# Attention with an exact-Gelu MLP on one core: four raw weight pieces in flight instead of two, half of them staged in the turning buffers, and other portions of the MLP in the second batch

## Chip, cores, metric

One Trainium2 chip, one core. The metric is the device time of one execution in microseconds. A single execution's trace can differ from the next in its first 40 us by some microseconds (first loads), so totals are compared by medians over several runs, and traces by what happens inside them.

## The reference, cut to what matters

```python
# q, k, v: (8 batches, 8 heads, 576, 64) float32; tau = 0.02
scores = scale * np.matmul(q, k.transpose(0, 1, 3, 2))
thresh = np.max(scores, axis=-1, keepdims=True) - tau
scores = np.where(scores >= thresh, scores, -1000000000.0)
attn = exp(scores - max); attn = attn / (sum + 1e-09)
x = (attn @ v) as (4608 tokens, 512)
h = x @ w_in                       # w_in (512, 2048), handed in as float64
g = 0.5 * h * (1.0 + erf(h * inv_sqrt2))
return g @ w_out                   # w_out (2048, 512), handed in as float64
```

The weights come as 64-bit words; the kernel takes the words apart with integer steps and puts float32 together. That is done in 32 pieces of 128 x 512 values.

## The kernel before

The work is a row of *slots*. A pair of heads has five (four of 128 query rows for both heads, one for the tails), a batch has 20: slots 0 to 19 are batch 0, 20 to 39 batch 1. Each slot emits scores on TensorE, the softmax on VectorE and ScalarE, then some steps of the weights' conversion, then a portion of the MLP on TensorE. The order in the program is the order on each engine.

```python
    xg = ctx.enter_context(tc.tile_pool(name="xg", bufs=7))       # raw pieces AND blocks of x
    pd = [const.tile([P, 4 * KR, P], FP32, name=f"pd{e}") for e in range(2)]   # turning buffers
    # ...
    def load_piece():
        # ...
        raw, shifted = (xg.tile([P, 2 * PIECE], U32, tag="x", name=s) for s in ("raw", "shifted"))
        nc.gpsimd.dma_start(raw, src.bitcast(U32))
        n = 8 * PIECE - 4
        nc.gpsimd.dma_start(shifted.bitcast(U8)[:, 0:n], src.bitcast(U8)[:, 3:3 + n])
        raws.append((dst, raw, shifted))

    def conversions():
        ahead = None
        while raws or ahead:
            piece = None
            if raws:
                # ... expo of piece k+1 (VectorE), power of piece k+1 (ScalarE)
                vec.tensor_scalar(expo, hi, 0x7FF00000, None, op0=ALU.bitwise_and)
                nc.scalar.activation(power, expo, AF.Relu, bias=rebias, scale=8.0)
                piece = dst, hi, top, power
                yield 450
            if ahead:
                # ... mant, power, product of piece k (VectorE); then the next load is emitted
                vec.tensor_scalar(mant, top, 0x0FFFFFFF, 0x10000000, op0=ALU.bitwise_and, op1=ALU.bitwise_or)
                yield 450
                vec.scalar_tensor_tensor(power, hi, 0x80000000, power, op0=ALU.bitwise_and, op1=ALU.bitwise_or)
                yield 720
                vec.scalar_tensor_tensor(dst, mant, 2.0 ** -28, power.bitcast(FP32), op0=ALU.mult, op1=ALU.mult)
                load_piece()
                converted[0] += 1
                yield 720
            ahead = piece

    # turn_p, late batches: the weights p of a slot are turned into pd; after the fourth slot
    # pd is stored to DRAM, from where it comes back in another order
        to = pd_tail[p % 2] if i == NC else pd[e][:, :, i * Q:(i + 1) * Q]
        nc.vector.transpose(to[:, 0:NB, :], w[:, e * S:(e + 1) * S].rearrange("p (b i) -> p b i", i=Q))
    # ...
    goal = [0.0] + [1.5 + 2.08 * i for i in range(B - 1)]     # blocks of the MLP done by the end of a batch
    for n in range(len(slots) + WEIGH + 1):
        # ... scores, softmax_head, turn_p of the slot before, softmax_tail, loads
        if n < BATCH:
            convert(2300)
        elif batch < 2:
            convert(9000)
        if n >= BATCH:
            done = min(batch, B - 1)
            fill((goal[done] - goal[done - 1]) * BLK_NS / (BATCH if done > 1 else BATCH), weighed // HP)
```

`convert(ns)` runs conversion steps until their estimated times (the yields) sum to ns; `fill(ns)` does the same with the matmuls of the MLP. A block of the MLP is 256 tokens: 64 hT matmuls, eight Gelus, 32 o_ps matmuls (the trace has two instructions for each float32 matmul).

Names in the profile: sc are scores, p the weights that softmax makes of them, hT and o_ps the first and the second product of the MLP, g its Gelu; raw and shifted are the two copies of a piece's words that are loaded, expo, mant and power the steps of its conversion (exponent bits, mantissa bits, signed power of two).

## Time and profile before

| | before |
|---|---|
| median of 4 runs beside the changed kernel | 1530.50 us (1530.03 to 1532.71) |
| span of the profiled run | 1528.7 us |
| TensorE busy | 94% |
| TensorE idle up to slot 19 / slots 19 to 24 / slots 24 to 39 | 36.1 / 41.6 / 8.2 us |

The last row is the sum of the gaps that TensorE's timeline shows ahead of its lines, split at the scores of the tail slots. After slot 39 there are none, so idle time before it (and slow-clock time that follows idle time) is what this change can win. The prediction shows the lines themselves.

### The profile page before, as it was taken

What the parts mean: (1) busy time and instruction counts of PE and PEld (TensorE: products, weight loads), DVE (VectorE), ACT (ScalarE), POOL (GpSimd) and SP (SyncE); (2) the same over time, 40 slices, a digit from 0 to 9 for tenths busy, and PEclk for the clock granted to TensorE, in tenths of its full rate; (3) what the DMA queues carried; (4) which work ended last, traced back from release to release, by engine and by line L of the source; (5) the groups of instructions that cost most, each with busy time, mean ns of one, the idle gap of its engine ahead of it and who ended that gap; (6) DMA issues with size and microseconds to landing.
All of it is one profiled execution on the core that took longest, in us unless ns stands there. A gap on an engine that the chain in (4) does not pass through costs nothing.

```text
span 1528.7 us, 17454 instructions
## 1 busy us (share of the span) xinstructions
PE 1438.7 (94%) x6092; PEld 897.3 (59%) x6092; DVE 899.7 (59%) x2089; ACT 643.3 (42%) x934; POOL 40.9 (3%) x84
## 2 busy tenths in 40 slices
PE   6875558999999999999999999999999999999999
PEld 4443444665656565757565757575747474765764
DVE  6997566667676667676776666667666666000000
ACT  5775364563535252625362635262626252100110
POOL 3112100000000000000000000000000000000000
PEclk9888679999999999999999999999999999999999
DMA  9665457777666667676776767666666655500000
GB/s 257 177 201 183 146 157 180 186 179 187 175 170 177 179 162 185 174 198 172 182 185 180 183 173 181 152 167 169 178 179 174 172 150 147 144 14 7 7 14 14
DMA packets 398887, 237.61 MB, mean 155 GB/s; under 512 B 230352, under 2 KB 380880, under 8 KB 391632
## 3 DMA queue, kind: packets, MB, share of 16 engines
q1 hardware_dynamic: 391632, 202.96, 51.5%
q0 software_dynamic: 7168, 33.54, 6.5%
q8 instruction: 49, 0.80, 0.2%
q14 instruction: 38, 0.31, 0.1%
HBM read 144.43 MB, written 92.01 MB: 155 GB/s over the span
## 4 chain that ended last, share of the span: by engine, by line
PE 82%; issue 9%; DMA 3%; POOL 2%; ACT 1%; DVE 1%; SPq 0%; POOLq 0%; DVEq 0%; ACTq 0%
PE o_ps L430 32%; PE hT L419 31%; PE sc L313 10%; PE xT L391 9%; DMA shifted<-in_moe_w_in_dram 1%; POOL raw L136 1%; DMA turned<-pd 1%; POOL shifted L138 1%; DVE p L338 1%; SPq L366 0%; DMA shifted<-in_moe_w_out_dram 0%; ACT L325 0%; ACT L423 0%; ACT p L347 0%; DVE nmx L324 0%
## 5 line engine op out<-in xcount | busy, mean ns | idle before, releaser
L419 PE MATMUL hT<-x,w_in 128*128 128x256 f32 x2304 | 525.1, 385 | 11.8 <-ACT x L400 11.8
L430 PE MATMUL o_ps<-w_out,g 128*128 128x512 f32 x1152 | 515.3, 599 | 0.0
L419 PEld LDWEIGHTS hT<-x,w_in 128*128 128x128 f32 x2304 | 438.2, 192 | 100.5 <-issue 27.9
L324 DVE TENSOR_REDUCE nmx<-sc 128x1 f32<-128x576 f32 x288 | 206.2, 752 | 298.7 <-PE sc L313 297.6
L430 PEld LDWEIGHTS o_ps<-w_out,g 128*128 128x128 f32 x1152 | 215.1, 190 | 259.7 <-issue 256.9
L325 ACT ACTIVATE p<-sc,nmx 128x576 f32<-128x576 f32 x288 | 202.6, 741 | 335.8 <-DVE nmx L324 335.4
L338 DVE SCALAR_TENSOR_TENSOR p<-sc,thr,p 128x576 f32<-128x576 f32 x288 | 220.2, 796 | 19.4 <-ACT p L325 18.0
L313 PE MATMUL sc<-kT,qT 64*128 64x288 f32 x1024 | 183.3, 448 | 33.0 <-DVE p L338 32.8
L313 PEld LDWEIGHTS sc<-kT,qT 64*128 64x128 f32 x1024 | 102.0, 194 | 117.5 <-issue 100.2
L361 DVE STREAM_TRANSPOSE pd<-p 128x576 f32<-128x576 f32 x224 | 161.8, 757 | 10.7 <-DMA turned<-pd 10.7
L391 PE MATMUL xT<-pT,v 128*64 128x288 f32 x1280 | 165.9, 413 | 0.0
L423 ACT ACTIVATE g<-hT 128x512 f32<-128x512 f32 x144 | 85.0, 597 | 125.7 <-PE hT L419 124.8
L391 PEld LDWEIGHTS xT<-pT,v 128*64 128x64 f32 x1280 | 89.9, 139 | 76.5 <-issue 18.3
L349 DVE TENSOR_SCALAR p<-p,rden 128x576 f32<-128x576 f32 x216 | 103.6, 518 | 4.2
L423 ACT ACT_TABLE_LOAD x75 | 96.2, 1283 | 12.7 <-PE hT L419 11.6
L325 ACT ACT_TABLE_LOAD x74 | 94.9, 1283 | 1.6 <-DVE nmx L324 0.2
L400 ACT COPY x<-xT 128x256 f32<-128x256 f32 (+7 forms) x128 | 29.2, 282 | 152.3 <-PE xT L391 152.2
L433 ACT COPY o_sb<-o_ps 128x512 f32<-128x512 f32 x36 | 21.0, 584 | 147.7 <-PE o_ps L430 147.7
L347 ACT ACTIVATE p<-p,rden 128x576 f32<-128x576 f32 x72 | 52.4, 770 | 54.9 <-DVE rden L343 54.2
L313 PE MATMUL sc<-kT,q_tail 128*128 128x288 f32 x128 | 43.7, 468 | 30.2 <-DVE p L338 30.2
L313 PEld LDWEIGHTS sc<-kT,q_tail 128*128 128x128 f32 x128 | 23.7, 206 | 47.4 <-issue 43.3
L159 ACT ACTIVATE power<-expo,rebias 128x512 uint32<-128x512 uint32 x32 | 22.9, 717 | 46.2 <-DVE expo L158 46.2
(58 smaller groups left out, 431.1 us busy)
## 6 DMA issues: line engine op xcount, KB each, us to landing
pT<-turned SPq DMA_DIRECT2D x56, 1440.0 KB, 7.8
turned<-pd SPq DMA_DIRECT2D x224, 320.0 KB, 5.2
out_dram<-o_sb SPq DMA_DIRECT2D x36, 256.0 KB, 2.2
turned<-pd_tail SPq DMA_DIRECT2D x112, 80.0 KB, 2.9
raw<-in_moe_w_in_dram POOLq DMA_DIRECT2D x16, 512.0 KB, 5.1
raw<-in_moe_w_out_dram POOLq DMA_DIRECT2D x16, 512.0 KB, 3.9
shifted<-in_moe_w_in_dram POOLq DMA_DIRECT2D x16, 511.5 KB, 5.3
shifted<-in_moe_w_out_dram POOLq DMA_DIRECT2D x16, 511.5 KB, 4.5
```

Of the source, the lines that this page charges most:

```text
L313: nc.tensor.matmul(sc[e][:, h, 0:HALF], lhsT=lhsT, rhs=s["kT"][rows, at:at + HALF], start=True, stop=True)
L324: nc.vector.tensor_reduce(nmx[:, e:e + 1], sc, axis=AXIS.XY, op=ALU.max, negate=True)
L325: nc.scalar.activation(w[:, e * S:(e + 1) * S].rearrange("p (h s) -> p h s", h=2), sc, AF.Exp, bias=nmx[:, e:e + 1], scale=1.0)
L338: nc.vector.scalar_tensor_tensor(row, sc[e][:, :, 0:HALF], thr[:, e:e + 1], row, op0=ALU.is_ge, op1=ALU.mult, accum_out=den[:, e:e + 1])
L347: nc.scalar.activation(row, row, AF.Copy, bias=0.0, scale=rden[:, e:e + 1])
L349: nc.vector.tensor_scalar(row, row, rden[:, e:e + 1], None, op0=ALU.mult)
L361: nc.vector.transpose(to[:, 0:NB, :], w[:, e * S:(e + 1) * S].rearrange("p (b i) -> p b i", i=Q))
L391: nc.tensor.matmul(xT[f, 0:HALF], lhsT=s["v"][:, e, c, :], rhs=pT[:, c, cols], start=(c == 0), stop=(c == KR - 1))
L400: nc.scalar.copy(x_blk[n][:, hp, o:o + size], xT[:, at - lo:at - lo + size])
L419: nc.tensor.matmul(hT[:, j % 2, :], lhsT=w_in_sb[c][:, j * P:(j + 1) * P], rhs=x_blk[n][:, c, :], start=(c == 0), stop=(c == N_DM - 1))
L423: nc.scalar.activation(t, hT, AF.Gelu)
L430: nc.tensor.matmul(o[:, 0:d_model], lhsT=g[j][:, m * P:(m + 1) * P], rhs=w_out_sb[j], start=(j == 0), stop=(j == N_DF - 1))
```

## The change

Its intent: keep VectorE supplied with raw weights, so that 24 of 32 pieces are converted in batch 0, and give TensorE its first half block of the MLP early. The pool of seven tiles cannot hold four raw pieces (eight tiles) beside three blocks of x. The turning buffers are not needed before slot 21, so every second of the first 24 pieces is staged there.

```diff
+    EARLY_PIECES = 24
@@ load_piece
-        raw, shifted = (xg.tile([P, 2 * PIECE], U32, tag="x", name=s) for s in ("raw", "shifted"))
+        k = loaded[0] - 1
+        if k % 2 and k < EARLY_PIECES:
+            room = pd[k // 2 % 2][:, 0:NB - 2, :].bitcast(U32).rearrange("p b i -> p (b i)")
+            raw, shifted = room[:, 0:2 * PIECE], room[:, 2 * PIECE:4 * PIECE]
+        else:
+            raw, shifted = (xg.tile([P, 2 * PIECE], U32, tag="x", name=s) for s in ("raw", "shifted"))
@@ conversions: estimates of the steps 450, 450, 720, 720 -> 340, 340, 720, 700
@@ before the slots
-    for _ in range(2):
+    for _ in range(4):
         load_piece()
@@ in the slots
-        if n < BATCH:
-            convert(2300)
-        elif batch < 2:
-            convert(9000)
-        if n >= BATCH:
+        if batch == 0:
+            convert(EARLY_PIECES * 2100 / BATCH)
+        elif n < BATCH + 2:
+            convert(1e12 if n > BATCH else 9000)
+        if batch:
             done = min(batch, B - 1)
-            fill((goal[done] - goal[done - 1]) * BLK_NS / (BATCH if done > 1 else BATCH), weighed // HP)
+            share = (goal[done] - goal[done - 1]) * BLK_NS / BATCH
+            if batch == 1:
+                share = BLK_NS / 8 if n < BATCH + 4 else (share * BATCH - BLK_NS / 2) / (BATCH - 4)
+            fill(share, weighed // HP)
```

More of the change, by code (lines that the diff above doesn't have):

```diff
@@ L160, in conversions @@
                 piece = dst, hi, top, power
-                yield 450
+                yield 340
             if ahead:
@@ L165, in conversions @@
                 vec.tensor_scalar(mant, top, 0x0FFFFFFF, 0x10000000, op0=ALU.bitwise_and, op1=ALU.bitwise_or)
-                yield 450
+                yield 340
                 vec.scalar_tensor_tensor(power, hi, 0x80000000, power, op0=ALU.bitwise_and, op1=ALU.bitwise_or)
@@ L171, in conversions @@
                 converted[0] += 1
-                yield 720
+                yield 700
             ahead = piece
```

## The prediction

> **What bounds the kernel now.** I read the page's 40 slices first, then busy time in stretches of 20 us, then the waits of the first 320 us, then the timelines of VectorE and TensorE where the stretches show trouble. The slices come first because the averages of the span hide two regimes:
>
> ```profile
> PE   6875558999999999999999999999999999999999
> DVE  6997566667676667676776666667666666000000
> PEclk9888679999999999999999999999999999999999
> ```
>
> One digit is 38 us. From the ninth slice on TensorE is full; only before it, in some 310 us, can time be had. The change touches only this part: attention of batch 0, conversion of the 32 weight pieces (their float64 words are turned into float32 on VectorE, with one step on ScalarE), and the slots of batch 1. Stretches:
>
> ```profile
> 120.00:140.00 20.00, 12.44 (x63) 8.03 (x63) 17.24 (x44) 11.76 (x20) 3.22 (x6) 0.83 0.66 188
> 140.00:160.00 20.00, 8.21 (x39) 5.38 (x37) 11.35 (x25) 5.79 (x12) 4.40 (x8) 0.72 0.59 198
> 160.00:180.00 20.00, 12.18 (x53) 9.59 (x51) 10.36 (x22) 5.78 (x8) 3.75 (x7) 0.84 0.52 184
> 180.00:200.00 20.00, 8.87 (x28) 6.50 (x28) 10.22 (x22) 7.13 (x10) 3.31 (x7) 0.67 0.30 105
> 240.00:260.00 20.00, 20.00 (x86) 9.54 (x86) 13.30 (x32) 8.62 (x17) 0.00 (x0) 1.00 0.48 101
> ```
>
> Columns after the length: busy us of PE, PEld, DVE, ACT, POOL, then granted clock, DMA share, GB/s. Up to 140 VectorE is the bound (17 to 19 of 20 us from 40 on). Between 140 and 205 nothing is: VectorE half idle, TensorE half idle and slow, DMA far from full. That is a chain of latencies, and the waits name it:
>
> ```profile
> POOL raw L136 <- DVE mant L165: 123.6, 24, 14.4
> DVE expo L158 <- DMA raw<-in_moe_w_out_dram: 26.7, 10, 3.9
> ```
>
> One turn of the chain in VectorE's timeline:
>
> ```profile
> 145.03 0.43 DVE L158 TENSOR_SCALAR expo<-raw 128x512 uint32<-128x512 uint32 x1 [2.87 <-DMA raw<-in_moe_w_out_dram]
> 145.37 0.42 DVE L165 TENSOR_SCALAR mant<-shifted 128x512 uint32<-128x512 uint32 x1
> 145.70 0.69 DVE L167 SCALAR_TENSOR_TENSOR power<-raw,power 128x512 uint32<-128x512 uint32 x1
> 146.42 0.69 DVE L169 SCALAR_TENSOR_TENSOR w_out<-mant,power 128x512 f32<-128x512 uint32 x1
> 149.90 0.43 DVE L158 TENSOR_SCALAR expo<-raw 128x512 uint32<-128x512 uint32 x1 [2.78 <-DMA raw<-in_moe_w_out_dram]
> ```
>
> Two pieces are in flight, but the order on VectorE is expo of piece k+1 before mant of piece k. Only mant frees the buffer for load k+2, and expo of k+2 is the very next thing after piece k. So each load is waited for in full: 4.87 us a piece, of which 2.8 is waiting. TensorE hangs on this, in order:
>
> ```profile
> 156.36 10.56 PE L419 MATMUL hT<-x,w_in 128*128 128x256 f32 x34 [11.79 <-ACT x L400]
> 183.98 2.99 PE L313 MATMUL sc<-kT,qT 64*128 64x288 f32 x8 [11.81 <-DVE p L338]
> 208.93 2.26 PE L313 MATMUL sc<-kT,q_tail 128*128 128x288 f32 x4 [16.08 <-DVE p L338]
> ```
>
> These three gaps are 39.7 us. After 216 idle time on TensorE comes to only some 8 us more (0.78, 0.99, 1.01, 3.68, 0.19, 1.51).
>
> **What the Trainium skill says.** (1) "DMA: Bandwidth & Descriptors", Anatomy of one DMA (SWDGE path): some 2.0 us fixed plus bytes over 436e3 per us, so 3.2 us for a raw half of 512 KB. The trace has 3.8 us as its least and 4.1 as its median from issue to landing of raw: a little slower, same order, and mostly latency, so depth is the right cure. (2) Same page, Queues, rings and completion order: each engine takes turns between queue rows, packet by packet. So a deeper weight queue takes turns from the q, k, v loads; the trace agrees in that the k load of pair 1 is waited for until 28.8 us while DMA share is 0.9 to 1.1. (3) "TensorE: Matmul & The Clock Gate", What's actually happening: after an idle window the array runs at half clock until it has been busy. The trace agrees: the same eight sc matmuls take 2.99 us at 184 and 1.24 us at 253.7. Gaps cost more than their length. (4) "Perfetto Trace Analysis", Optimization Strategy: a bubble that recurs unchanged can mean too few buffers; the 2.8 us bubble is that.
>
> **The change, part by part.** Slots are numbered 0 to 19 for batch 0, 20 to 39 for batch 1.
>
> *More conversion in batch 0.* From the order of instructions: when slot 20's softmax ends, 24.2 pieces are through VectorE instead of 19.7. A piece takes 1.94 us start to start (expo 0.34, mant 0.34, power 0.6 to 0.7, product 0.6). 4.5 x 1.94 = +8.7 us on the engine that bounds this part. Small waits for raw disappear there (0.40, 0.59, 0.20, 0.51, 0.28: -2.0). The first loads now are 4 MB rather than 2 MB beside q, k, v on a saturated DMA: I allow +2 us. Slot 20's softmax ends at 139.5 + 8.7 = 148 instead of 139.5.
>
> *Fewer pieces afterwards, but not deeper.* From piece 24 on everything is in the pool of 7 again, of which 3 hold x; four pieces in flight would need 8. The order of GpSimd's DMA issues with their waits shows it: load 25 waits for the buffers of piece 22, 26 for 24's, 27 for 25's, up to 31 for 29's. So 24 and 25 are there in time, and 26 to 31 run at the old cadence, 4.87 us each. Waits of 2.8 us: 6 instead of 9. Laid out: expo 26 at 152.9, 27 at 157.8, 28 at 162.6, 29 at 167.5; slot 21's softmax (4.8 us as before) to 172.7; expo 30 at 177.2, expo 31 at 182.1, the last two products to 185.7. Before, the last product ended at 211.2, after slot 23's softmax. Four conversions now stand between slots 20 and 21 as before did three, and ScalarE's copy of x is behind five power steps in order: the first hT starts at about 169 (before 156.4).
>
> *Larger portions.* An eighth of a block per slot for slots 20 to 23 rather than 0.075: 16 matmuls (32 instructions; the trace has two per matmul) instead of some 10. At slot 21 two portions are due: 64 instructions from 169, at 0.31 us cold for the first 34 as at 156.4 and 0.23 after, to 187. Then slots 22 and 23: 1.24 for sc and 7.3 us for 32 hT each, longer than VectorE's 5 to 7 us, so TensorE has no gap. sc of slot 24 starts at 203.7 with 128 hT done (before 208.9 with 78), sc of slot 25 at about 208.7 with the work of 144 (before 216.25 with 96). Lead: 7.5 us + 48 x 0.23 = 18.5 us.
>
> *Smaller portions in slots 24 to 39.* 0.0625 block instead of 0.075: 3.6 us instead of 4.6 a slot. Now the serial chain of a slot bounds more of them. Where a Gelu stands in it the trace's period is 7.44 us:
>
> ```profile
> 222.88 1.94 PE L313 MATMUL sc<-kT,qT 64*128 64x288 f32 x8 [0.78 <-DVE p L338]
> ...
> 230.31 1.94 PE L313 MATMUL sc<-kT,qT 64*128 64x288 f32 x8 [0.99 <-DVE p L338]
> ```
>
> Eight of the 16 slots hold a Gelu (hT of block 1), eight hold o_ps. TensorE's work in slots 25 to 39: sc 18.6, xT 15.2, MLP 15 x 3.6 = 54, sum 88 us; before 103 less the MLP difference of 15, that is 98 warm, and it took 114 (216.25 to 330). The chain makes it some 99 to 106 now. So idle plus cold time there is 11 to 18 against 16 before: between +5 and -2 of the lead is kept or lost.
>
> *Sum.* Lead 18.5 us, less 4 us for slots 25 to 39 and for what I may have put too early in the first 40 us. Gain about 14 us. From slot 40 on TensorE is full in both kernels and emits the same work, so the lead goes through to the end: 1530 - 14 = 1516 us.
>
> **The rivals.** *The whole serial stretch goes*: if four pieces really were in flight up to the last, the six waits (17 us) would go too, and time would be near 1499. The intent speaks for it; the buffers' waits in the instruction order speak against it. *The bound moves and nothing is won*: VectorE pays 8.7 us more up front and DMA contention delays pair 1's k more than I allow; slots 25 to 39 turn chain-bound at 7.4 us each (16 x 7.4 + 3 x 3 = 127 us would be worse than before). VectorE's 95% busy share in 40 to 60 us speaks for the first; that the slots with o_ps ran at 5.7 us speaks against the second. It would give 1524 to 1530. *The portions alone do it*: the new loads bring nothing net, since 8.7 us up front eats the saved waits (3 x 2.8 = 8.4), and the gain is only the hT done early in slots 20 to 23, which would otherwise stand still. By my own sum this is nearly so; it gives the same 1512 to 1520, but says where the gain is from.
>
> **Range and chances.** Batch 0's end is uncertain by 4 us, slots 25 to 39 by 6, slot 20 to 24 by 4; as independent errors about 8 us. That gives 1506 to 1526. Over 2% faster means below 1499.4, which needs the first rival: 0.06. Over 2% slower would need a new stall of 45 us: 0.01. Within 2%: 0.93.
>
> **What would show it right or wrong.** Right: six waits of expo for raw of 2.7 to 3.9 us in about 150 to 185; slot 20's softmax ending at 146 to 150; hT starting near 169 and TensorE without a gap over 1 us from there to 205; small gaps of 0.5 to 2 us in slots 25 to 39. Wrong: waits of VectorE for raw in batch 0 over 4 us in sum (contention), fewer than five late waits (depth after all), or gaps in slots 25 to 39 that sum to over 18 us.

## The result, and the profile after

The changed kernel: median 1520.06 us of 4 runs (1518.85 to 1522.02), against 1530.50 before. The ratio is 0.993, 95% interval 0.9913 to 0.9947: 0.7% faster.

First the page's slices of the changed kernel; one digit is 38 us of its 1520.2:

```profile
PE   5877588999999999999999999999999999999998
DVE  6998566676666676676677766666666676000000
PEclk9797798999999999999999999999999999999999
```

Beside the line of before: the fourth slice went from 5 to 7 and the sixth from 5 to 8, with VectorE at 7 and 6 there before and at 8 and 6 after. TensorE is at 9 from the eighth slice on in both kernels (the prediction counts it as the ninth), so the difference must lie in the first seven.

The stretches of 20 us of the changed kernel (same columns as in the prediction: length, PE, PEld, DVE, ACT, POOL, clock, DMA share, GB/s) show both sides:

```profile
140.00:160.00 20.00, 12.11 (x65) 6.48 (x65) 13.81 (x34) 7.07 (x12) 3.21 (x6) 0.88 0.43 150
160.00:180.00 20.00, 10.99 (x43) 9.45 (x44) 10.84 (x23) 5.58 (x11) 3.75 (x7) 0.69 0.45 159
180.00:200.00 20.00, 17.90 (x79) 13.68 (x78) 12.99 (x27) 13.21 (x18) 0.67 (x2) 0.91 0.19 64
...
220.00:240.00 20.00, 16.52 (x60) 8.07 (x62) 13.94 (x33) 7.91 (x12) 0.00 (x0) 0.83 0.81 209
240.00:260.00 20.00, 15.59 (x58) 7.24 (x54) 10.80 (x24) 6.83 (x13) 0.00 (x0) 0.94 0.71 165
```

From 180 to 200 TensorE is busy 17.90 us instead of 8.87: the stretch that the change was made for. From 240 to 260 it is busy 15.59 instead of 20.00: time is given back in a stretch that was full. The waits of the first 320 us name both ends (us in total, times, longest):

```profile
POOL pd L143 <- DVE power L174: 58.1, 10, 10.3
POOL raw L143 <- DVE mant L172: 58.0, 11, 10.1
...
DVE expo L165 <- DMA raw<-in_moe_w_out_dram: 17.1, 6, 3.0
POOL shifted L145 <- DVE power L174: 17.0, 3, 7.1
...
DVE pd L368 <- DMA turned<-pd: 10.3, 3, 4.2
```

GpSimd's waits for a free buffer fell only from 157 us (123.6 for raw, 33.3 for shifted) to 133: those for raw alone halve, but the staged pieces now have waits of their own, under the name pd. GpSimd is merely further ahead when it waits. What counts is VectorE's wait for the words: 29.2 us in 15 before (26.7 of it in the line that the prediction shows), 17.5 in 7 after. Six of the seven are late ones; two of them in VectorE's timeline:

```profile
152.66 0.43 DVE L165 TENSOR_SCALAR expo<-raw 128x512 uint32<-128x512 uint32 x1 [2.67 <-DMA raw<-in_moe_w_out_dram]
...
157.53 0.43 DVE L165 TENSOR_SCALAR expo<-raw 128x512 uint32<-128x512 uint32 x1 [2.78 <-DMA raw<-in_moe_w_out_dram]
```

The period is 4.87 us still: four in flight holds only as long as the turning buffers can be used. TensorE's timeline carries the rest:

```profile
169.01 14.41 PE L426 MATMUL hT<-x,w_in 128*128 128x256 f32 x58 [14.35 <-ACT x L407]
...
185.52 0.81 PE L426 MATMUL hT<-x,w_in 128*128 128x256 f32 x2 [2.10 <-ACT g L430]
...
204.62 1.13 PE L320 MATMUL sc<-kT,q_tail 128*128 128x288 f32 x4
209.12 1.75 PE L320 MATMUL sc<-kT,qT 64*128 64x288 f32 x8
...
223.48 2.99 PE L320 MATMUL sc<-kT,qT 64*128 64x288 f32 x8 [4.18 <-DVE p L345]
...
260.70 2.99 PE L320 MATMUL sc<-kT,qT 64*128 64x288 f32 x8 [5.11 <-DVE p L345]
```

After six hT instructions at 153.10 the next wait for ScalarE's copy of x until 169.01; the copy stands on ScalarE behind the power step of the fourth late wait (167.97 to 168.69). Then TensorE has work up to slot 25, whose scores start at 209.12 (before: 216.25). After that come gaps of 4.18 and 5.11 us, each followed by scores that take 2.99 us instead of 1.24 (granted clock 0.52 from 223.4 to 226.4). The scores wait for VectorE's p of the slot before; VectorE in turn waited here:

```profile
217.37 0.78 DVE L368 STREAM_TRANSPOSE pd<-p 128x576 f32<-128x576 f32 x1
221.85 0.78 DVE L368 STREAM_TRANSPOSE pd<-p 128x576 f32<-128x576 f32 x1 [3.70 <-DMA turned<-pd]
```

This is the first transpose of a pair into its turning buffers. The second of the two waits 3.70 us until the store of the pair before (out of the same buffer) has been read. SyncE's timeline shows that store's issue:

```profile
207.51 10.40 SPq L373 DMA_DIRECT2D turned<-pd  x8
```

Eight transfers take 10.40 us to be issued, from 207.51 to 217.91, and the buffer is free at 221.85: 14.3 us after the first issue. Between the last writing of a buffer and the next pair's first there are two slots. Slots of some 7.5 us cover most of that (before, VectorE waited here for 7.0 us in three, between 139 and 335 us); shorter portions make shorter slots, and the same stretch has 11.5 us in four. e8_swap tests this reading.

TensorE's idle time by part, by the same sums as in the table of before:

| idle us on TensorE | before | changed |
|---|---|---|
| up to slot 19 | 36.1 | 41.5 |
| slots 19 to 24 | 41.6 | 19.4 |
| slots 24 to 39 | 8.2 | 12.9 |
| sum | 85.9 | 73.8 |

The sum falls by 12.1 us; the medians fell by 10.4, and the two executions profiled differ by 8.5 (1528.7 and 1520.2).

### The profile page after: what moved, and what is told of

Same layout as the page of the kernel before. It is cut to its first block, busy times and chain, and to the rows that moved or that the text cites. A ratio compares the mean times of both kernels' runs of the same rounds, so it can differ in the third digit from the quotient of the medians.

```text
span 1520.2 us, 17439 instructions
## 1 busy us (share of the span) xinstructions
PE 1442.4 (95%) x6092; PEld 899.0 (59%) x6092; DVE 900.2 (59%) x2089; ACT 640.4 (42%) x932; POOL 41.3 (3%) x84
## 4 chain that ended last, share of the span: by engine, by line
PE 86%; DVE 6%; issue 3%; SPq 2%; ACT 2%; DMA 2%; POOL 0%; POOLq 0%; ACTq 0%; DVEq 0%
PE hT L426 33%; PE o_ps L437 32%; PE sc L320 11%; PE xT L398 9%; DVE p L345 2%; DVE nmx L331 1%; DVE power L174 1%; DMA turned<-pd 1%; DVE w_in L176 1%; DMA k<-in_k_dram 1%; SPq L228 1%; ACT p L332 1%; SPq L224 1%; DVE expo L165 0%; SPq L373 0%
## 5 line engine op out<-in xcount | busy, mean ns | idle before, releaser
L426 PE MATMUL hT<-x,w_in 128*128 128x256 f32 x2304 | 524.0, 385 | 16.4 <-ACT x L407 14.3
L320 PEld LDWEIGHTS sc<-kT,qT 64*128 64x128 f32 x1024 | 103.4, 197 | 115.5 <-issue 96.2
L430 ACT ACT_TABLE_LOAD x74 | 94.9, 1283 | 12.7 <-PE hT L426 11.6
L332 ACT ACT_TABLE_LOAD x73 | 93.7, 1283 | 3.1 <-DVE nmx L331 1.7
L407 ACT COPY x<-xT 128x256 f32<-128x256 f32 (+7 forms) x128 | 29.2, 284 | 150.4 <-PE xT L398 150.4
L335 DVE TENSOR_SCALAR thr<-nmx,tau_eff 128x2 f32<-128x2 f32 (+1 forms) x160 | 36.2, 226 | 5.7
```

The lines of the kernel that those rows point to most:

```text
L320: nc.tensor.matmul(sc[e][:, h, 0:HALF], lhsT=lhsT, rhs=s["kT"][rows, at:at + HALF], start=True, stop=True)
L332: nc.scalar.activation(w[:, e * S:(e + 1) * S].rearrange("p (h s) -> p h s", h=2), sc, AF.Exp, bias=nmx[:, e:e + 1], scale=1.0)
L335: nc.vector.tensor_scalar(thr[:, 0:n], nmx[:, 0:n], -1.0, tau_eff, op0=ALU.mult, op1=ALU.subtract)
L426: nc.tensor.matmul(hT[:, j % 2, :], lhsT=w_in_sb[c][:, j * P:(j + 1) * P], rhs=x_blk[n][:, c, :], start=(c == 0), stop=(c == N_DM - 1))
L430: nc.scalar.activation(t, hT, AF.Gelu)
```

## The experiments

Theory A is the one formed after reading the two traces: the new loads and the larger portions each help a part of slots 20 to 24, the six late waits remain because staging ends at piece 24, and part of the gain is lost in slots 25 to 39 because their portions became too short. Rivals: portions alone do it; loads alone do it; the losses come from contention. All outputs are right. Each kernel was timed against the kernel before on the same chip, e1 to e4 on one and the others on a second. For e9 to e12 nine of the ten runs of the kernel before are those of the call before, on that same chip.

| label | kernel | us | before | ratio (95%) |
|---|---|---|---|---|
| e1_portions | before, portions of the change | 1527.06 | 1529.46 | 0.9981 (0.9969 to 0.9994) |
| e2_loads | change, portions of before | 1516.80 | 1529.46 | 0.9912 (0.9898 to 0.9926) |
| e3_deeper | change, staging to piece 28 | 1508.57 | 1529.46 | 0.9856 (0.9838 to 0.9874) |
| e4_spread | change, last pieces spread | 1507.81 | 1529.46 | 0.985 (0.9831 to 0.9869) |
| c1_after | the change again | 1517.17 | 1528.16 | 0.9927 (0.9914 to 0.9940) |
| e5_later | change, 1.8 blocks in batch 1 | 1515.20 | 1528.16 | 0.9912 (0.9899 to 0.9926) |
| e8_swap | change, turning after softmax | 1512.18 | 1528.16 | 0.9890 (0.9876 to 0.9903) |
| e7_all | several together | 1495.62 | 1528.16 | 0.9787 (0.9773 to 0.9800) |
| e9_portions17 | change, 1.7 blocks in batch 1 | 1510.75 | 1528.41 | 0.9891 (0.9871 to 0.9911) |
| e10_best | e7_all with 1.7 | 1490.37 | 1528.41 | 0.9749 (0.9735 to 0.9762) |
| e11_less_early | e10_best, 20 pieces in batch 0 | 1497.10 | 1528.41 | 0.9795 (0.9781 to 0.9808) |
| e12_two_in_flight | change, two in flight | 1537.61 | 1528.41 | 1.0062 (1.0047 to 1.0077) |

### The two halves of the change

**e1_portions**: the kernel before with only the new portions.

```diff
-            fill((goal[done] - goal[done - 1]) * BLK_NS / (BATCH if done > 1 else BATCH), weighed // HP)
+            share = (goal[done] - goal[done - 1]) * BLK_NS / BATCH
+            if batch == 1:
+                share = BLK_NS / 8 if n < BATCH + 4 else (share * BATCH - BLK_NS / 2) / (BATCH - 4)
+            fill(share, weighed // HP)
```

> The kernel before with the larger portions alone: an eighth of a block in slots 20 to 23, 0.0625 after; loads and conversion as before. Theory A (both parts give; the loads shorten the serial stretch): slot 24 is reached at about 209 us as before, but with 128 instead of 78 hT instructions, slot 25 near 213, slots 25 to 39 take 112 us as in the changed kernel, total about 1524 us, that is 4 us more than the changed kernel. Rival B (the loads bring nothing net, the portions do it all): the same as the changed kernel, 1518 to 1521 us. Rival C (the portions do nothing): 1530 us.

Measured: 0.2% faster. That is not the 6 us of theory A but 2 to 3. TensorE's timeline of this kernel shows what becomes of the larger portions without the loads:

```profile
179.78 1.22 PE L419 MATMUL hT<-x,w_in 128*128 128x256 f32 x2 [9.65 <-ACT g L423]
```

The fifth hT buffer waits 9.65 us for a Gelu (there are four), and ScalarE has the Gelu behind power steps that wait for VectorE. The same comes once more, 8.45 us at 207.03. Idle time between slots 19 and 24 is 33.7 us, 41.6 before. The matmuls were offered earlier, but could not be done earlier by as much.

**e2_loads**: the change with uniform portions.

```diff
-            if batch == 1:
-                share = BLK_NS / 8 if n < BATCH + 4 else (share * BATCH - BLK_NS / 2) / (BATCH - 4)
```

> The changed kernel with uniform portions of 0.075 block as before; loads and conversion as changed. Theory A: slot 25 at about 209 us with only the hT of 96, so a lead of 7 us instead of 18, slots 25 to 39 in 112 to 114 us: about 1523 us. Rival B (the loads bring nothing net): 1529 to 1531 us. Rival C (the loads do it all): 1518 to 1521 us.

Measured: 1516.80 us, 0.9% faster. This is as fast as the change itself and below the 1518 to 1521 of rival C, so theory A was wrong on this point and the rival that the loads do it all was right. TensorE's timeline has the tail slot 24 early:

```profile
195.80 1.21 PE L320 MATMUL sc<-kT,q_tail 128*128 128x288 f32 x4
```

With all portions at 0.075 the slots 22 and 23 are short on TensorE, VectorE has no conversion left in them, and slot 24 starts at 195.8 rather than 204.6 (with less MLP work done: 78 hT instructions rather than 128). From slot 24 on the gaps are smaller than the change's (8.4 us rather than 12.9), because the later portions were not cut.

**c1_after**, the change once more, in the call with e5, e8 and e7 (no edit):

> The changed kernel once more, beside the others of this call on one chip, as the loads-alone run came out lower than it on another chip. If the larger portions help: 1513 to 1517 us here. If they are worth nothing on top of the loads: a ratio to the kernel before of 0.990 to 0.993.

Measured: ratio 0.9927, beside 0.9912 of e2_loads. The intervals overlap: on top of the loads no gain of the changed portions is seen.

**e12_two_in_flight**: is it the depth, or only the faster rate of conversion that came with it?

```diff
-        if k % 2 and k < EARLY_PIECES:
+        if False:
-    for _ in range(4):
+    for _ in range(2):
         load_piece()
```

> The changed kernel's rate of conversion (24 pieces in batch 0) and portions, but two pieces in flight, all in the pool, nothing in the turning buffers. Theory A (the faster rate needs the depth: where two expo steps fall in one slot the second waits for a load issued just before): two waits of 2 to 3 us in every five slots of batch 0, some 18 us in all, slot 20's softmax ends near 165 us, total 1531 to 1537 us, slower than the kernel before. Rival B (the slots' softmax hides the loads anyhow; the rate alone is the gain): waits in batch 0 under 6 us, total 1516 to 1521 us.

Measured: 0.6% slower than the kernel before. Its waits up to 215 us:

```profile
DVE expo L165 <- DMA raw<-in_moe_w_out_dram: 25.9, 12, 3.1
DVE expo L165 <- DMA raw<-in_moe_w_in_dram: 11.6, 5, 3.7
```

37.5 us in 17 waits, rather than 17.1 in 6. Asking for 24 pieces in batch 0 with two buffers only moves the waiting into batch 0 (20.7 us of it). So the faster rate does not pay without the depth: shown. The other half, four in flight at the old rate, was not run.

### What is left on the path of the conversion

**e3_deeper**: pieces 25 and 27 staged in the turning buffers too (pieces count from 0 and only odd ones are staged, so the bound at 28 adds those two).

```diff
-        if k % 2 and k < EARLY_PIECES:
+        if k % 2 and k < EARLY_PIECES + 4:
```

> The changed kernel with pieces 25 and 27 staged in the turning buffers too, so that four are in flight until piece 28. Theory A (each late load is waited for in full since only two buffers are left): the waits for raw of pieces 26, 27, 28 vanish, 29 shrinks below 1 us, only 30 and 31 keep 2.4 to 2.9 us; sum 5 to 7 instead of 17.1 us; hT starts near 158 instead of 169 us, total about 1509 us. Rival (bandwidth or GpSimd's issuing sets the cadence of 4.9 us a piece): six waits stay, 1518 to 1521 us. Rival (waits vanish, but the lead is lost in slots 25 to 39): waits as in A, total 1516 to 1520 us.

Measured: 1508.57 us, as theory A had it (1509). Waits between 139 and 335 us, then the first hT:

```profile
DVE expo L165 <- DMA raw<-in_moe_w_out_dram: 6.5, 3, 3.0
```

```profile
156.05 12.79 PE L426 MATMUL hT<-x,w_in 128*128 128x256 f32 x58 [2.24 <-ACT x L407]
```

Three waits instead of six, 6.5 us instead of 17.1, and the first hT 13 us earlier (169.01 to 156.05; 2.3 of these are there at slot 19 already, by an earlier end of the first loads). The ratio is 0.9856 beside c1_after's 0.9927, some 11 us. That is the causal chain of the prediction, taken one step further than the change went.

**e4_spread**: instead of converting the last eight pieces in two blocks of four, in slots 20 and 21, two per slot.

```diff
-        elif n < BATCH + 2:
-            convert(1e12 if n > BATCH else 9000)
+        elif n < BATCH + 5:
+            convert(1e12 if n > BATCH + 3 else 4200)
```

> The changed kernel with the last eight pieces converted two in each of slots 20 to 23, instead of four in slot 20 and four in slot 21; loads as changed. Theory A (the burst of conversions with its waits stands in front of slot 21's softmax and of the copies of x): three waits of 2.8 us instead of six, hT starts near 154 instead of 169 us, slot 25 near 200 instead of 209 us, total about 1511 us. Rival (VectorE is the bound in slots 20 to 24 whatever the order): slot 25 at 207 to 209 us, total 1518 to 1521 us.

Measured: 1507.81 us, better than the 1511 expected. The first hT no longer has five pieces ahead of it:

```profile
151.59 12.79 PE L426 MATMUL hT<-x,w_in 128*128 128x256 f32 x58 [1.25 <-ACT x L407]
```

It starts at 151.59, and its wait is 1.25 us rather than 14.35. Slot 25 starts at about 194 rather than 209. The raw words are still waited for (9.1 us in 3), but softmax and TensorE's portions lie between.

### What is given back in slots 25 to 39

**e5_later**: batch 1 does 1.8 blocks rather than 1.5, so portions after slot 23 are longer.

```diff
-    goal = [0.0] + [1.5 + 2.08 * i for i in range(B - 1)]
+    goal = [0.0, 1.8] + [1.5 + 2.08 * i for i in range(1, B - 1)]
```

> The changed kernel with larger portions in slots 24 to 39: 1.8 blocks in batch 1 instead of 1.5, so 0.081 block a slot instead of 0.0625, and the less in batch 2. Theory A (what the first slots' lead lost was lost since a pair of heads cannot go faster than some 37.4 us there, whatever the portion, through the store of the turned tile and the chain of a slot): a pair still takes 37 to 39 us, the gaps of TensorE of 4.2 and 5.1 us shrink below 3, 0.3 block (17 us) is done for little, total 10 to 14 us less than the changed kernel of the same chip. Rival B (the gaps are caused by the chain and stay as they are, TensorE's work comes on top): a pair takes 41 us, total within 2 us of the changed kernel.

Measured: only 2 us against c1_after rather than 10 to 14, and the intervals overlap. That is rival B's total, but not its mechanism (pairs of 41 us). The part that theory A spoke of went as expected: pairs take 37.9 to 39.1 us and the gaps of 4.18 and 5.11 become 2.2 each. The gain is lost elsewhere. TensorE's timeline past slot 40:

```profile
342.17 2.79 PE L320 MATMUL sc<-kT,qT 64*128 64x288 f32 x8 [2.77 <-DVE p L345]
...
354.15 13.98 PE L426 MATMUL hT<-x,w_in 128*128 128x256 f32 x64
```

The input of block 2 is not finished before slot 43 (576 rows of batch 0 hold two blocks of 256). With 1.8 blocks done at slot 40 only 0.2 are left for four slots; TensorE runs dry (gaps of 1.03 and 2.77 us, no hT at all), then a whole column of 64 hT at once. Before, it had no gaps there.

**e9_portions17** is the same with 1.7, which leaves 0.3 of a block for slots 40 to 43.

```diff
-    goal = [0.0] + [1.5 + 2.08 * i for i in range(B - 1)]
+    goal = [0.0, 1.7] + [1.5 + 2.08 * i for i in range(1, B - 1)]
```

> The changed kernel with 1.7 blocks in batch 1: an eighth of a block in slots 20 to 23 as changed, and 0.075 a slot after, as in the kernel before. With 1.8 the trace showed TensorE running out of finished x in slots 41 to 43 (only two blocks of x exist until slot 43); 1.7 stays below. Theory A (the early lead was real, and the smaller portions after it gave it back as idle and cold time): idle time of TensorE in slots 24 to 39 falls from 13 to about 8 us, no gap after slot 40, total 4 to 6 us less than the changed kernel, a ratio of 0.988 to 0.990 to the kernel before. Rival B (portions do not matter once the loads are changed): 0.991 to 0.993.

Measured: ratio 0.9891, below c1_after's 0.9927 without overlap of the intervals. Idle time in slots 24 to 39 is 6.9 us rather than c1_after's 12.7, and one gap of 0.53 us is left after slot 40. So with the eighths in slots 20 to 23 the later portions should not be cut for them (0.075 here as before). Beside e2_loads (0.9912) the intervals overlap: that the eighths themselves are worth something is not shown.

**e8_swap**: keeps the short portions and takes the wait for the store off the path: in a pair's second slot, turning into the buffers comes after softmax, not before.

```diff
-        if 0 < n <= len(slots):
+        late_turn = n > BATCH and i == 1 and p < NP
+        if 0 < n <= len(slots) and not late_turn:
             (turn_p if n > BATCH else turn_p_early)(*slots[n - 1])
@@ after softmax_tail
+        if late_turn:
+            turn_p(*slots[n - 1])
```

> The changed kernel with one order changed: in the second slot of a pair, from slot 21 on, the transposes into the turning buffers stand after the slot's threshold step instead of before it, so that VectorE's wait for the store no longer holds back the scores' buffers. Theory A (the store's wait in front of the threshold step makes TensorE's gaps of 4.2 and 5.1 us): those gaps go below 2 us, total 3 to 6 us less than the changed kernel of the same chip. Rival (VectorE is behind anyhow, the gap only moves one slot on): within 2 us of it.

Measured: 5 us faster than c1_after, within theory A's 3 to 6. Waits from 139 to 460 us, first of c1_after, then of e8_swap:

```profile
DVE pd L368 <- DMA turned<-pd: 12.3, 6, 4.4
```

```profile
DVE pd L368 <- DMA turned<-pd: 3.7, 2, 2.2
```

12.3 us become 3.7. The store takes as long as before (14.3 us from its first issue at 203.27 until the buffer is free); it is merely no longer in front of softmax. The two large gaps shrink from 4.0 and 5.3 us to 2.3 and 2.9, not below 2 as expected; slots 24 to 39 take 106.7 us rather than 110.3, with a mean granted clock of 0.95 rather than 0.91. So the wait for the store is shown to be a cause of the gaps, but not the only one; the two transposes themselves (0.78 us each) left softmax's way with it, and their share was not taken apart.

### The version that beats both

**e7_all**: e4_spread, piece 25 staged in a turning buffer as well (not 27: with the pieces spread out it would be converted after turning has begun), 1.8 blocks, and the swap.

```diff
-        if k % 2 and k < EARLY_PIECES:
+        if k % 2 and k < EARLY_PIECES + 2:
@@ and the edits of e4_spread, e5_later and e8_swap
```

> All that seems to help at once: the last eight pieces two per slot, piece 25 staged in the turning buffers too, 1.8 blocks in batch 1 with an eighth in each of the first four slots, and the transposes after the threshold step in each pair's second slot. If the parts add: 1508 (two per slot) less 12 (portions) less 3 (order) less 2 (one wait fewer): about 1491 us. If the portions and the order cure the same gaps: about 1494 us. If the gain is capped as VectorE bounds slots 20 to 39: 1500 us or more.

Measured: 1495.62 us, 2.1% faster than before, and nearest to the 1494 of "the same gaps". Slots 40 to 43 are starved again as in e5_later (5.3 us idle between slots 39 and 44).

**e10_best**: the same with 1.7.

```diff
-    goal = [0.0, 1.8] + [1.5 + 2.08 * i for i in range(1, B - 1)]
+    goal = [0.0, 1.7] + [1.5 + 2.08 * i for i in range(1, B - 1)]
```

> The kernel with all that helped, with 1.7 instead of 1.8 blocks in batch 1. If the 5.3 us of gaps between slots 40 and 44 there came from x not yet being finished: those gaps go, 1490 to 1493 us. If they came from elsewhere: 1495 to 1498 us.

Measured: 1490.37 us (1488.29 to 1492.70), 2.5% faster than before. The page's slices:

```profile
PE   5777999999999999999999999999999999999998
PEclk8877999999999999999999999999999999999999
```

TensorE is at 9 from the fifth slice on, rather than the eighth, with its clock at 9 there too. Between slots 19 and 44 its gaps sum to 11.4 us, 5.6 up to slot 24, 3.9 up to slot 39 and one of 1.9 after. So of e7_all's 5.3 us after slot 39 most went with the smaller portion, not all. What is left lies ahead of slot 19 (41.2 us), where VectorE is the bound (85.7 of 92 us busy from 40 to 132).

**e11_less_early**: e10_best with 20 pieces in batch 0 and twelve afterwards, two per slot; the half block in six twelfths.

```diff
-            convert(EARLY_PIECES * 2100 / BATCH)
-        elif n < BATCH + 5:
-            convert(1e12 if n > BATCH + 3 else 4200)
+            convert(20 * 2100 / BATCH)
+        elif n < BATCH + 7:
+            convert(1e12 if n > BATCH + 5 else 4200)
-                share = BLK_NS / 8 if n < BATCH + 4 else (share * BATCH - BLK_NS / 2) / (BATCH - 4)
+                share = BLK_NS / 12 if n < BATCH + 6 else (share * BATCH - BLK_NS / 2) / (BATCH - 6)
@@ staging: k < 22
```

> The same with 20 pieces instead of 24 converted in batch 0, the other twelve two per slot in slots 20 to 25, and the first half block in six portions of a twelfth. Theory A (up to slot 25 VectorE's total sets the time, so 8 us moved from before slot 20 to after it change nothing): slot 20's softmax ends near 140 us, slot 26 at the same time within 3 us, total within 3 us of the kernel beside it. Rival B (conversion beside the MLP is cheaper than in batch 0, as TensorE has work then): 5 to 8 us less.

Measured: 6.7 us slower than e10_best; both theories missed. Slot 19 starts 7 us earlier (125.07 rather than 132.17) and that is lost again:

```profile
174.03 2.26 PE L320 MATMUL sc<-kT,q_tail 128*128 128x288 f32 x4 [9.00 <-DVE p L345]
...
200.16 2.99 PE L320 MATMUL sc<-kT,qT 64*128 64x288 f32 x8 [4.96 <-DVE p L345]
```

Gaps of 9.00 and 4.96 us ahead of the scores, which wait for VectorE's p. VectorE waits 15.1 us for raw words in five waits (5.6 in two in e10_best), since more of the pieces fall after the staging's end. Which part of the 6.7 us is due to these waits and which to the smaller portions was not taken apart.

## Why the prediction was right or wrong

The time was right: 1516 predicted, 1520.06 measured, inside the range. By its steps:

- **Batch 0.** Right here, in part by luck. Softmax of slot 20 ended at 148.0 (148 predicted, 139.6 before), and only 0.42 us of waits for raw remained in batch 0. The allowance of 2 us for contention came true in this execution: the last k of pair 1 was waited for until 30.95 us instead of 28.77. In eight other executions profiled with this batch 0 (e2 to e10 in the table) that k was there by 28.8 and the same softmax ended at 144.6 to 145.8, below the predicted 146 to 150; in c1_after k came at 32.00 and it ended at 149.1. What decides this was not looked into. The timestamps in the next points share this luck, the lengths do not.
- **Six late waits.** Right in number and spacing, here to a fraction of a microsecond: expo 26 to 31 at 152.66, 157.53, 162.51, 167.45, 177.27 and 182.31; 17.1 us in sum. The buffers decided, and the first rival (all waits go) fell. e3_deeper shows the cause.
- **First hT at 169.** Right (169.01).
- **No gap over 1 us up to 205.** Wrong by one gap of 2.10 us at 185.52: the 33rd hT matmul needs a fifth hT buffer and waits for a Gelu. The prediction did not count that pool of four. It cost little; slot 24 came at 204.62 (203.7 predicted).
- **The lead at slot 25.** Right in size: 216.25 - 209.12 = 7.1 us, and 48 x 0.23 = 11 us of work done ahead, 18.1 together (18.5 predicted). Where it comes from is another matter (last point).
- **Slots 25 to 39.** Wrong in size, and this is the term that was mis-sized. Predicted 99 to 106 us, measured 321.42 - 209.12 = 112.3. By the prediction's own 88 us of TensorE work that leaves 24 us: 12.9 are gaps, and the rest, some 11 by this estimate, is time at a lower clock after gaps (mean granted clock 0.89 there, 0.96 before; scores of 2.99 us that else take 1.24). It had reckoned with 11 to 18 of both, and with small gaps of 0.5 to 2 us; two gaps were 4.18 and 5.11. Two things failed. The sum for the kernel before is off (88 + 15 is 103, so of its 114 us 11 were lost, not 16); and the chain was read from the kernel before, where longer portions hid the wait for the store of the turning buffers. That wait was 7.0 us in three before, 7.1 in three with the new loads and the old portions (e2_loads), and 11.5 in four after (139 to 335 us). e8_swap shows that it costs time. At slot 40 the lead was 330.92 - 321.42 = 9.5 us, 8.6 less than at slot 25, where the prediction had set aside 4.
- **Where the gain comes from.** The third rival, "the portions alone do it", was given room by the prediction's own sum ("by my own sum this is nearly so"). It is wrong: e1_portions brings 0.2%, e2_loads 0.9%, the change 0.7%. The step that failed is the balance of the loads, "8.7 us up front eats the saved waits" (8.4): the 4.5 pieces that are converted in batch 0 are also missing later, so slots 20 to 24 save the 8.7 as well as the waits, 17.1 together. In e2_loads slot 19 came 5.7 us later than before (132.81 and 127.11), but slot 24 followed after 63.0 us instead of 81.8 (18.8 saved), so it came 13.1 us earlier, with the same 78 hT instructions done; at slot 40 a lead of 14.5 us was left. The portions were not free either: with them slot 24 followed slot 19 after 69.4 us, 6.4 more than in e2_loads, and slots 24 to 39, with their smaller portions, gave back only 3.4 (112.2 us, not 115.5).

So a total within 4 us of the measured one held a loss that was put 4 to 5 us too small and a wrong account of where the gain is from; the total alone would not have shown either.

## What to carry to other kernels

A consumer that looks one piece ahead, and frees a buffer only behind that look, needs more than two buffers: with two, each load was waited for in full here (2.8 us of 4.87 a piece) wherever no other work of VectorE stood between two pieces, though the queue was far from full (DMA share 0.3 to 0.6). Time won ahead of a stage that has its own chain of latencies is partly given back there, so work out the period of the next stage with its shortened work, not with the old one. Move work forward only as far as its input reaches, and put a burst on one engine in small parts between the others' steps.

## What the Trainium skill lacked or had wrong

- "DMA: Bandwidth & Descriptors", Anatomy of one DMA: about 2 us fixed plus bytes over 436e3 per us, an estimate of 3.2 us for 512 KB (the prediction's 3.2 is this estimate). The changed kernel shows medians of 3.9 us from issue to landing for raw words of w_out in the pool, and for those of w_in, loaded while q, k and v are, 7.6 in the pool and 4.9 in the turning buffers. Each has a second load of the same size issued some 0.6 us after it, so this is a limit of the page's sum for one DMA, not a fault in it.
- "Perfetto Trace Analysis", Optimization Strategy: it tells that a recurring bubble can mean too few buffers; no page says how many are needed when the consumer works one piece ahead. The runs: two in flight at the higher rate 37.5 us of waits (e12_two_in_flight), four up to piece 24 17.1 us, up to piece 28 6.5 us (e3_deeper).
- "ScalarE: Activation LUTs", What ACT_TABLE_LOAD costs: 1283 ns for the load, which the trace has to the digit (mean 1283 ns of 74), and some 1380 ns of drain per switch, which it does not show: over 147 loads of the changed kernel the median gap on ScalarE is 0.02 us before the load and 0.02 after it. At 183.57 us, for one, the load starts 0.02 us after the ACTIVATE before it ended (182.83 + 0.72), and the next ACTIVATE follows at 184.87, 0.02 us after the load's end.
- No page that I found has the time until a buffer is free again after a store in many short rows: here eight stores of 320 KB took 10.40 us to issue and held the buffer for 14.3 us from the first issue.
